# All matmuls of a convolution and gated MLP moved into two 64-row lanes

## Chip, cores and metric

One core of one Trainium2 chip. The metric is the device time of one execution in microseconds (us), the median of several executions. In the lines of the profile, PE is TensorE, PEld its weight loads, ACT is ScalarE, DVE is VectorE, POOL is GpSimd and SPq the DMA queue of SyncE.

## The reference

A depthwise causal convolution with 7 softmax-normalised taps per head, then `g = h * cos(h)` between two matrix products, over 32768 tokens:

```python
# convolution: x is 8 x 4096 x 192, weight is 8 heads x 7 taps; each head has 24 channels
w = softmax(weight)                       # over the 7 taps, 1e-9 in the denominator
out = np.einsum('hk,bskhg->bshg', w, x_unf)   # x_unf: the 7 last tokens of each token
# then, on out as 32768 x 192:
h = x @ w_in                              # 192 x 2048
g = h * np.cos(h)
return g @ w_out                          # 2048 x 192
```

## The kernel before

The 8 batches are handled as 4 pairs; `s` is the half of a pair. Every group of 448 tokens (a unit) is convolved on TensorE with a band matrix per head, copied to bf16, and transposed by DMA into `cT`. Then 512 steps, each 128 of the 2048 hidden columns for 2 x 512 tokens, run `up`, `sin` (ACT) and `mult` (DVE), and 19 steps later a sixteenth of the down-projection of 2 x 512 tokens. The 192 channels do not fit in 128 rows: channels 0 to 127 are a 128-row matmul, the other 64 are 64-row matmuls, one for each `s`, in the two halves of the array. The cuts of code below are shortened.

```python
h_pool = tc.tile_pool(name="hps", bufs=3, space=PSUM)   # 2 banks each
m_pool = tc.tile_pool(name="mps", bufs=1, space=PSUM)   # misc[0..1], convolution and down share them
...
def up(n):                                    # one step
    h = h_pool.tile([128, 2, T], FP32, name="h")
    for s in range(2):                        # 128 rows
        nc.tensor.matmul(out=h[:, s, :], lhsT=wA[:, f * 128:(f + 1) * 128], rhs=cT[b][:, s, t0:t0 + T],
                         start=True, stop=False)
    for s in range(2):                        # 64 rows: rows 0-63 for s=0, 64-127 for s=1
        p = slice(s * DR, (s + 1) * DR)
        nc.tensor.matmul(out=h[:, s, :], lhsT=wR[p, f * 128:(f + 1) * 128], rhs=cT[b][p, 2, t0:t0 + T],
                         start=False, stop=True)

def down(m):                                  # 8 matmuls of 128 rows and 192 columns
    ...
    for f in range(fh * 8, fh * 8 + 8):
        nc.tensor.matmul(out=bank[:, jj * D:(jj + 1) * D], lhsT=gs[i * NF + f][:, s, tk], rhs=wo[:, f, :],
                         start=(f == 0), stop=(f == NF - 1))

for k in range(6):
    conv_part(misc[k % 2])
for n in range(NSTEP + LAG):                  # LAG = 19
    m = n - LAG
    if n % 4 == 1: conv_part(misc[((m // 4) + 1) % 2])
    if n < NSTEP: up(n); sin(n)
    if m >= 0: down(m)
    if 1 <= n <= NSTEP: mult(n - 1)
```

The band matrices are built at the start by 8 x 7 DVE operations on seven masks.

## Time and profile before

| | before |
|---|---|
| median | 870.2 us (869.85 to 870.95, 3 runs) |
| TensorE, DVE, ACT busy | 93%, 80%, 74% |
| first up, first down, last down (start) | 53.8, 79.9, 864.8 us |
| one step in the full stretch | 1.52 us |

The last two rows are read from the starts of TensorE's instructions. The durations that the profile gives for matmuls overlap (247 ns on average for 192 columns, with starts 83 ns apart), so their sum exceeds the time on the clock. Only differences of starts give the pace. The prediction shows the lines.

### The profile page before, as it was taken

What the parts mean: (1) busy time and instruction counts of PE and PEld (TensorE: products, weight loads), DVE (VectorE), ACT (ScalarE), POOL (GpSimd) and SP (SyncE); (2) the same over time, 40 slices, a digit from 0 to 9 for tenths busy, and PEclk for the clock granted to TensorE, in tenths of its full rate; (3) what the DMA queues carried; (4) which work ended last, traced back from release to release, by engine and by line L of the source; (5) the groups of instructions that cost most, each with busy time, mean ns of one, the idle gap of its engine ahead of it and who ended that gap; (6) DMA issues with size and microseconds to landing.
All of it is one profiled execution on the core that took longest, in us unless ns stands there. A gap on an engine that the chain in (4) does not pass through costs nothing.

```text
span 869.1 us, 16182 instructions
## 1 busy us (share of the span) xinstructions
PE 811.0 (93%) x6744; PEld 474.2 (55%) x6744; DVE 694.6 (80%) x656; ACT 642.4 (74%) x685; POOL 59.5 (7%) x51
## 2 busy tenths in 40 slices
PE   0158999999999999999999999999999999999998
PEld 0013555555565556555555555555555555555557
DVE  1959888888888888888888888888888888888782
ACT  2048777777877777778777777787777778778773
POOL 1210010010000010100000000010000000000000
PEclk9999999999999999999999999999999999999999
DMA  7242332342332423433233334333332221011101
GB/s 208 76 109 67 93 101 59 94 117 78 93 90 76 126 65 88 110 90 90 76 90 98 88 79 122 88 84 84 94 91 76 59 55 37 20 37 38 38 31 61
DMA packets 128217, 71.20 MB, mean 82 GB/s; under 512 B 55440, under 2 KB 127632, under 8 KB 128144
## 3 DMA queue, kind: packets, MB, share of 16 engines
q1 hardware_dynamic: 128144, 70.18, 29.2%
q8 instruction: 52, 0.85, 0.4%
q14 instruction: 21, 0.17, 0.1%
HBM read 32.40 MB, written 25.17 MB: 66 GB/s over the span
## 4 chain that ended last, share of the span: by engine, by line
PE 91%; DVE 5%; DMA 2%; ACT 1%; issue 1%; SPq 0%; ACTq 0%
PE misc L262 45%; PE h L234 25%; PE h L238 18%; DVE band L144 3%; PE misc L161 2%; DVE g L249 2%; DMA st<-in_moe_w_in_dram 1%; PE misc L171 1%; DMA cT<-ct 0%; DVE ct L223 0%; ACT cos L244 0%; PE misc L168 0%; DVE band L142 0%; PE misc L204 0%; PE misc L163 0%
## 5 line engine op out<-in xcount | busy, mean ns | idle before, releaser
L249 DVE TENSOR_TENSOR g<-h,cos 128x1024 bf16<-128x1024 f32 x512 | 625.1, 1223 | 128.5 <-ACT cos L244 122.8
L244 ACT ACTIVATE cos<-h,halfpi 128x1024 bf16<-128x1024 f32 x512 | 569.6, 1113 | 172.4 <-PE h L238 167.3
L262 PE MATMUL misc<-wo,g 128*128 128x192 bf16 x4096 | 423.5, 247 | 0.0
L262 PEld LDWEIGHTS <-g 128*128 128x128 bf16 x4096 | 312.7, 98 | 111.6 <-issue 111.6
L234 PE MATMUL h<-cT,wA 128*128 128x512 bf16 x1024 | 305.7, 380 | 10.8 <-DMA cT<-ct 5.9
L238 PE MATMUL h<-cT,wR 64*128 64x512 bf16 x1024 | 200.1, 388 | 0.0
L238 PEld LDWEIGHTS <-wR 64*128 64x128 bf16 x1024 | 49.1, 93 | 217.7 <-issue 217.7
L234 PEld LDWEIGHTS <-wA 128*128 128x128 bf16 x1024 | 88.3, 98 | 15.0 <-DMA cT<-ct 6.6
L100 POOL CAST xb<-xw 128x1536 bf16<-128x1536 f32 x32 | 46.9, 1465 | 483.4 <-DMA xw<-in_x_dram 453.9
L267 ACT COPY osb<-misc 128x384 f32<-128x384 f32 x128 | 60.2, 470 | 10.3 <-PE misc L262 10.3
L161 PE MATMUL misc<-xb,band 128*128 128x96 bf16 x360 | 28.8, 211 | 37.2 <-DVE band L144 36.9
L223 DVE CAST ct<-misc 112x512 bf16<-112x512 f32 (+1 forms) x74 | 50.8, 687 | 10.6 <-PE misc L163 0.7
L161 PEld LDWEIGHTS <-band 128*128 128x128 bf16 x360 | 22.6, 100 | 39.2 <-DVE band L144 37.5
L221 ACT CAST ct<-misc 112x512 bf16<-112x512 f32 (+1 forms) x38 | 21.7, 572 | 27.0 <-PE misc L163 27.0
L144 DVE SCALAR_TENSOR_TENSOR band<-mask,wn,band 128x128 bf16<-128x128 bf16 x48 | 21.4, 445 | 1.7
L171 PE MATMUL misc<-xb,band 128*128 128x192 bf16 x72 | 12.4, 252 | 3.5 <-DVE halfpi L276 2.1
L163 PE MATMUL misc<-xb,band 128*128 128x32 bf16 x72 | 13.1, 182 | 2.2 <-DVE band L144 2.2
L129 DVE TENSOR_REDUCE wsum<-wex 128x8 f32<-128x56 f32 x1 | 0.2, 210 | 13.8 <-ACT wex L127 13.8
L95 POOL CAST xb<-xw 128x1536 bf16<-128x1536 f32 x4 | 5.9, 1463 | 61.6 <-DMA xw<-in_x_dram 43.3
L115 ACT CAST wA<-st 128x1024 bf16<-128x1024 f32 x2 | 2.1, 1044 | 10.1 <-DMA st<-in_moe_w_in_dram 10.1
L163 PEld LDWEIGHTS <-band 128*128 128x128 bf16 x72 | 7.2, 101 | 2.4 <-DVE band L144 2.4
L168 PE MATMUL misc<-xb,band 128*128 128x128 bf16 x36 | 8.0, 222 | 0.3 <-ACT ct L221 0.2
(26 smaller groups left out, 30.6 us busy)
## 6 DMA issues: line engine op xcount, KB each, us to landing
xw<-in_x_dram SPq DMA_DIRECT2D x64, 384.0 KB, 4.1
out_dram<-osb SPq DMA_DIRECT2D x64, 384.0 KB, 2.6
xw<-in_x_dram SPq DMA_DIRECT2D x8, 336.0 KB, 4.2
cT<-ct SPq DMA_TRANSPOSE x112, 2.4
st<-in_moe_w_out_dram SPq DMA_DIRECT2D x2, 768.0 KB, 8.9
st<-in_moe_w_in_dram SPq DMA_DIRECT2D x2, 512.0 KB, 9.1
st<-in_moe_w_in_dram SPq DMA_DIRECT2D x4, 256.0 KB, 7.1
xw<-in_x_dram SPq DMA_DIRECT2D x8, 60.0 KB, 2.4
```

Of the source, the lines that this page charges most:

```text
L100: nc.gpsimd.tensor_copy(out=xb, in_=xw)
L144: nc.vector.scalar_tensor_tensor(out=band[:, h, :], in0=mask[:, k, :], scalar=wn[:, h, k:k + 1], in1=band[:, h, :], op0=ALU.mult, op1=ALU.add)
L161: nc.tensor.matmul(out=ps[:, :, h * G:(h + 1) * G], lhsT=band[:, h, :], rhs=xb[:, s, 0:nb, h * G:(h + 1) * G], start=True, stop=True)
L171: nc.tensor.matmul(out=ps[:, :, :, h * G - DA:(h + 1) * G - DA], lhsT=band[:, h, :], rhs=xr[:, :, :, h * G:(h + 1) * G], start=True, stop= ...
L221: nc.scalar.copy(ct[0:rows, 0:cols], bank[0:rows, 0:cols])
L223: nc.vector.tensor_copy(out=ct[0:rows, 0:cols], in_=bank[0:rows, 0:cols])
L234: nc.tensor.matmul(out=h[:, s, :], lhsT=wA[:, f * 128:(f + 1) * 128], rhs=cT[b][:, s, t0:t0 + T], start=True, stop=False)
L238: nc.tensor.matmul(out=h[:, s, :], lhsT=wR[p, f * 128:(f + 1) * 128], rhs=cT[b][p, 2, t0:t0 + T], start=False, stop=True)
L244: nc.scalar.activation(out=cos, in_=hs[n], func=AF.Sin, bias=halfpi, scale=1.0)
L249: nc.vector.tensor_tensor(out=g, in0=hs.pop(n), in1=cs.pop(n), op=ALU.mult)
L262: nc.tensor.matmul(out=bank[:, jj * D:(jj + 1) * D], lhsT=gs[i * NF + f][:, s, tk], rhs=wo[:, f, :], start=(f == 0), stop=(f == NF - 1))
L267: nc.scalar.copy(osb[i][:, 2 * p:2 * p + 2, :].rearrange("p a d -> p (a d)"), bank[:, 0:2 * D])
```

## The change

Its intent is that TensorE never changes its row mode, that is between 128-row and 64-row matmuls. The time lost at such a change is called a drain below. All of them become 64-row matmuls in two lanes, rows 0 to 63 and rows 64 to 127, which alternate in the program. In the up-projection each lane takes one `s` and has its own PSUM bank. In the convolution and the down-projection the two lanes hold the two halves of one sum, so they first write one bank each and then trade banks. A trade waits for a one-element GpSimd memset that waits for the last matmul before it. The order of work comes from a string that is repeated once per 8 steps. The band goes to DRAM as rows and comes back with each row shifted. The convolution now takes its PSUM from the three `h` buffers.

```diff
+    lane = (slice(0, L), slice(L, 128))          # L = 64
+    def lanes(a, b, after=None):
+        todo, at, ins = [list(a), list(b)], [0, 0], None
+        while todo[0] or todo[1]:
+            k = 0 if at[0] <= at[1] else 1       # the lane that is behind
+            ...
+            ins = nc.tensor.matmul(out=o, lhsT=w, rhs=r, start=start, stop=stop, skip_group_check=True)
+            if after is not None:
+                order(ins, after); after = None
+        return ins
+    def changeover(end):
+        ins = nc.gpsimd.memset(mark, 0.0)
+        order(ins, end)
+        return ins
     def up(n):
-        (two 128-row matmuls, two 64-row matmuls)
+        lanes(*[[(h[:, l, :], w1[lane[l], c, fc], cT[b][lane[l], c, tk], T, c == 0, c == NCH - 1)
+                 for c in range(NCH)] for l in range(2)])     # NCH = 3
     def down(m):
-        (eight 128-row matmuls)
+        def half(bank, l):                       # four matmuls of lane l
+            return [(acc[bank][:, t * D:(t + 1) * D],
+                     gs[f][lane[l], s, (2 * bank + t) * 128:(2 * bank + t + 1) * 128], w2[lane[l], f % NF, :], D, ...)
+                    for f in (f0, f0 + 1) for t in range(2)]
+        end = lanes(half(flip, 0), half(1 - flip, 1), state.pop("turn") if j == 8 else None)
+        if j == 7:
+            state["turn"] = changeover(end)
@@ band
-    (masks, 8 x 7 DVE operations)
+    nc.scalar.dma_start(out=rows_d, in_=taps)
+    nc.scalar.dma_start(out=band, in_=dram(rows_d, rows_d.offset + 127, [[ROW - 1, 128], [1, H * 128]]))
@@ start and order
+    for c in range(1, 4):
+        load_w1(c)                               # DMA and a GpSimd cast each
+    for u in (2, 3):
+        load_unit(0, u)
+    opened = [conv_first() for _ in range(3)]
+    relay = changeover(opened[2][3])
+    prepare()
+    (second halves, copies, transposes)
+    for c in range(4):
+        load_w2(c)                               # DMA and a GpSimd cast each
+    emit("USM" * 2 + ("CUScMe" + "USM" * 3) * 3 + "USM" * 2 + "U")
+    while count["y"] < 2 * NI:
+        emit("dddSMdUdMSdUdMSdUMdSUdSMdUdSMCdcdeMUdSdUyxUMS")
```

U is an up, S the cosine, M the multiply, d half a former `down`, C and c the two halves of a convolution, e its copy, x and y the stores of the two banks.

## The prediction

> **What bounds the kernel now.** I read the page from the top: engine shares, the chain that ended last, the groups. The engine line and the chain say TensorE:
>
> ```profile
> PE 811.0 (93%) x6744; PEld 474.2 (55%) x6744; DVE 694.6 (80%) x656; ACT 642.4 (74%) x685; POOL 59.5 (7%) x51
> ...
> PE 91%; DVE 5%; DMA 2%; ACT 1%; issue 1%; SPq 0%; ACTq 0%
> ```
>
> A busy TensorE is not a full one, so next come the groups and the waits. L234 and L238 are the up-projection (128 rows, then two 64-row pieces), L262 the down-projection, L249 and L244 the elementwise pair:
>
> ```profile
> L249 DVE TENSOR_TENSOR g<-h,cos 128x1024 bf16<-128x1024 f32 x512 | 625.1, 1223 | 128.5 <-ACT cos L244 122.8
> L244 ACT ACTIVATE cos<-h,halfpi 128x1024 bf16<-128x1024 f32 x512 | 569.6, 1113 | 172.4 <-PE h L238 167.3
> ...
> L238 PEld LDWEIGHTS <-wR 64*128 64x128 bf16 x1024 | 49.1, 93 | 217.7 <-issue 217.7
> ```
>
> DVE and ACT wait for PE, not the reverse. And the weight load of L238 sits still for 217.7 us with nothing to wait for. The timeline of TensorE in the middle of the run shows why (first column the start, second how long, both in us):
>
> ```profile
> 400.53 0.83 PE L262 MATMUL misc<-wo,g 128*128 128x192 bf16 x8
> 401.20 0.59 PE L234 MATMUL h<-cT,wA 128*128 128x512 bf16 x2
> 401.73 0.39 PE L238 MATMUL h<-cT,wR 64*128 64x512 bf16 x2
> 402.05 0.83 PE L262 MATMUL misc<-wo,g 128*128 128x192 bf16 x8
> 402.72 0.59 PE L234 MATMUL h<-cT,wA 128*128 128x512 bf16 x2
> ```
>
> Take starts, not durations. One step is 402.72 - 401.20 = 1.52 us: eight L262 in 0.67 us (83 ns each), L234 to L238 in 0.53 us, L238 to L262 in 0.32 us. Instruction by instruction in the trace, the second L234 starts 215 ns after the first (the streaming of 512 columns), but the first L238 comes 311 ns after the second L234: 96 ns more. The two L238 start 3 ns apart and run side by side, and the next L262 comes 319 ns later: 104 ns more than their 215 ns. So each step loses **0.20 us** where the array goes from 128 rows to 64 and back.
>
> The table by stretches gives the rest:
>
> ```profile
> 0.00:54.00 54.00, 4.87 (x31) 2.63 (x31) 27.45 (x74) 8.06 (x9) 8.74 (x12) 1.00 0.51 139
> 54.00:80.00 26.00, 21.13 (x109) 6.55 (x109) 22.43 (x21) 21.68 (x21) 3.83 (x3) 1.00 0.32 85
> 80.00:400.00 320.00, 320.00 (x2707) 188.50 (x2706) 268.54 (x238) 252.23 (x270) 25.12 (x20) 1.00 0.33 90
> ```
>
> (PE, weight loads, DVE, ACT, GpSimd, then clock, DMA share and GB/s.) Until 54 us TensorE does almost nothing: the band matrices are being built on DVE (48 instructions of 445 ns, after an exponential that queues behind weight casts on ACT until 18.8 us), then the first transposes land. From 54 to 80 us the pipeline fills, and DVE sets the pace. From 80 us TensorE has no gap up to 852 us; the last 160 L262 take 13.3 us. This adds up: 493 steps x 1.518 = 748 us, plus 24 us of convolution, is 772 = 852 - 80.
>
> **What the Trainium skill says.** "TensorEngine Tiling (Array Packing)", Key Properties: changing the tiling mode drains the TensorE. The trace agrees: 96 and 104 ns. The same page, Gotcha 1: different row tiles cannot access the same PSUM bank at once. That is why the change makes the lanes trade banks; nothing in this trace tests it. "TensorE: Matmul & The Clock Gate", Part 3, The mechanism: tiles in different row groups run together, about 4 ns apart. Agrees: 3 ns. The same section lets weight loads be pulled ahead of running matmuls where row groups differ, and Part 2 adds: or if they go to the background weight buffer. At 128 rows the trace shows it (the load for the next matmul starts 2 ns after the present one); in 64-row lanes no stretch of this trace has two matmuls of one lane in a row, so there it is **not shown**. This is the main risk.
>
> **The change part by part.**
>
> *Removed: the drains.* All matmuls become 64-row. 493 steps x 0.200 us = 99 us of TensorE time in the full stretch.
>
> *Lanes.* A U (up) has 3 matmuls of 512 columns in each lane: 3 x 215 = 0.648 us. A d (half as many columns of down as a step had) has 4 of 192 columns in each lane, 4 x 83 = 0.335 us, and each step has two. So a step is 0.648 + 0.670 = 1.318 us against 1.518. Matmuls go from 12 to 22 a step, but with pairs 3 ns apart and 24-column ones 25 ns apart in the trace, issue is no bound. The convolution stays at some 0.44 us for 2 x 512 columns in two lanes.
>
> *One pass of the order string* is 16 d, 8 U, one C and c: 16 x 0.335 + 8 x 0.648 + 0.44 = 10.98 us of TensorE. Is anything else longer? A cos takes 1113 ns, but starts 1.01 us after the one before where work is queued; 8 x 1.01 + a conv copy of about 1.0 + a store of 0.47 = 9.6 us of ACT. A multiply takes 1223 ns, but four of them in a row at 62.64 to 67.17 us give 1.13 us each; 8 x 1.13 + 0.45 = 9.5 us of DVE. Both are 13% below TensorE, though neither can be called idle.
>
> *PSUM buffers.* h has still three, and now the convolution uses them too. A buffer is held for 0.65 (U) + 0.21 (end of stream to ACT) + 1.11 + 0.03 + 1.22 + 0.05 = 3.27 us, a convolution for some 2.0 us: (8 x 3.27 + 2.0) / 3 = 9.4 us a pass. I walked the string by hand with these times: the tightest places are C and the U after it, where the buffer comes free within 0.02 us of its use; the rest have 0.14 to 0.8 us to spare. So the string fits, with little play. I add 0.1 us a pass for slips: 6 us.
>
> *The GpSimd marks.* A bank trade needs PE to GpSimd to PE, a few tenths of a us (a small memset is 0.10 us). At the eighth d a U of 0.65 us lies between, at the convolution a d of 0.335 us. Hidden, or nearly so; GpSimd is 7% busy.
>
> *Start.* Now the exponential waits for the weights alone (4.8 us), seven small DVE operations of about 0.2 us replace the mask and band work, and two DMAs through DRAM follow. With 2.4 to 4 us each (the landings of small DMAs on the page), band is there at about 16 us instead of 45 us. But the first conv is not the first up: the relay mark is on GpSimd behind the casts of four weight chunks, and each of these has 0.79 MB to load, since both lanes need a copy. Inputs before it are 0.89 + 0.79 + 4 x 0.79 = 4.8 MB; the old start moved 2.5 MB in 13 us, so 25 us, and 28 with the band's own traffic. Then three second halves, copies, and three transposes of double size (now 1.2 us of issue each, so about 2.4) with two x loads ahead of them on the queue: first U at about 38 us instead of 54. Gain 16 us.
>
> *Fill.* 17 steps and 3 convolutions before the first d instead of 19 steps and 5. DVE's pace, 17 x 1.13, or the buffers', gives 20 us. First d at 58 us.
>
> *Sum.* From then on TensorE has 495 U, 1024 d, 50 convolutions: 321 + 343 + 22 = 686 us. End of matmuls 58 + 686 + 6 = 750 us; the last store takes 4 us in the trace of before (865 to 869). 754 us in the span; with the odd microsecond between span and measured time and the tail of d's a little better covered, I say **752 us**, 14% less than 870.2.
>
> **Rivals.**
>
> *A: lanes expose their weight loads.* If a load in a lane has to wait for that lane's own matmul, each of the 16 x 4 + 8 x 3 + 8 = 96 matmuls of a lane in a pass costs perhaps 25 ns more (24-column matmuls with their loads are 25 ns apart, so one load takes no longer). 2.4 us a pass, 64 passes, 154 us: about 900 us, slower. For it: no evidence of prefetch in 64-row mode here. Against it: prefetch at 128 rows, and 64-row loads as short (93 ns) as 128-row ones (98 ns).
>
> *B: a new wait takes the drain's place.* Buffers or ACT and DVE stall TensorE, since everything now stands at 86% or more. A slip of 0.5 us a pass is 32 us: 780 us. The missing slack at C speaks for it; the string, evidently laid out for these times, against.
>
> *C: the start does not get shorter*, since the doubled w_in traffic replaces the band's work: 768 us. Or it gets better than I think (w_in lands sooner, first U at 28 us): 742 us.
>
> *D: double rate in lanes does not hold at 192 columns with a weight load each.* It would be like A.
>
> **Range and chances.** C and a small B give 728 to 790 as the 8-in-10 range. A or D at full size is what could make it slower than 870; I give that 4%, within 2% another 3%, faster by over 2% 93%.
>
> **What would show it.** In the new trace: pairs of matmuls 3 ns apart and pairs 83 or 215 ns apart without the 96 and 104 ns steps; passes of some 11 us; idle time of TensorE before C and U put down to DVE or ACT below 0.2 us a pass; first up-matmul near 38 us; DVE and ACT at about 90% in the full stretch. The prediction is wrong if pairs come at 105 ns or more (A, D), if TensorE waits for h over 0.5 us a pass (B), or if waits for GpSimd marks show up on TensorE.

## The result

| | before | changed |
|---|---|---|
| median | 870.58 us (869.85 to 871.15, 4 runs) | 760.17 us (759.12 to 760.4, 4 runs) |
| ratio | | 0.873 (95%: 0.8715 to 0.8745) |
| first up | 53.8 us | 33.3 us |
| first down | 79.9 us | 65.5 us |
| last down (start) | 864.8 us | 754.1 us |

So 20.5 us went from the start, the fill between first up and first down took 6.2 us more (32.3 against 26.1), and the stretch from first to last down shrank from 784.9 to 688.6 us, by 96.3 us. The page of the changed kernel, engine shares, chain and two groups:

```profile
PE 709.8 (94%) x12064; PEld 518.3 (68%) x12064; DVE 645.2 (85%) x592; ACT 589.8 (78%) x639; POOL 85.7 (11%) x247
...
PE 91%; DMA 4%; DVE 2%; ACT 1%; issue 1%; POOL 1%; SPq 1%; POOLq 0%; ACTq 0%
...
L309 DVE TENSOR_TENSOR g<-h,cos 128x1024 bf16<-128x1024 f32 x512 | 609.9, 1221 | 45.7 <-ACT cos L304 33.8
L304 ACT ACTIVATE cos<-h 128x1024 bf16<-128x1024 f32 x512 | 515.0, 1025 | 113.2 <-PE h L191 95.3
```

TensorE is still the bound, with 1.8 times as many matmuls. DVE used to wait 122.8 us for the cosine and now waits 33.8 us. Next, the timeline of TensorE in the middle of the run (start, length, then the group):

```profile
300.29 0.82 PE L191 MATMUL acc<-w,g 64*128 64x192 bf16 x16
300.95 0.81 PE L191 MATMUL h<-cT,w 64*128 64x512 bf16 x6
301.60 0.49 PE L191 MATMUL acc<-w,g 64*128 64x192 bf16 x8
301.93 0.81 PE L191 MATMUL h<-cT,w 64*128 64x512 bf16 x6
302.58 0.82 PE L191 MATMUL acc<-w,g 64*128 64x192 bf16 x16
```

Sixteen matmuls of 192 columns (two d) start within 0.66 us, 83 ns for each pair. An up takes 0.65 us, 215 ns for each pair. Nothing is lost between groups. The starts of the y stores are 11.02 us apart in the passes with a convolution and 10.46 us in those without.

The start and the fill are read from the timeline of the first 66 us:

```profile
28.10 1.46 PE L191 MATMUL h<-xb,band 64*128 64x192 bf16 x20 [7.22 <-POOL mark L201]
...
33.27 0.61 PE L191 MATMUL h<-cT,w 64*128 64x512 bf16 x2 [3.71 <-DMA cT<-ct]
...
44.89 0.82 POOL L169 CAST w<-so 128x768 bf16<-128x768 f32 x1 [1.15 <-DMA so<-in_moe_w_out_dram]
45.66 0.09 POOL L201 MEMSET mark<- 1x1 f32 x1
...
45.80 0.61 PE L191 MATMUL h<-xb,band 64*128 64x192 bf16 x6 [5.56 <-POOL mark L201]
...
52.10 0.40 PE L191 MATMUL h<-xb,band 64*128 64x64 bf16 x8
...
58.25 0.40 PE L191 MATMUL h<-xb,band 64*128 64x128 bf16 x6
```

Twice TensorE stood still for a GpSimd mark, 7.2 and 5.6 us. The second time the mark is a 0.09 us operation queued behind a cast that waited for its DMA. The last two lines show the rhythm of the fill: two convolutions 6.15 us apart, with four ups between them.

### The profile page after: what moved, and what is told of

It is laid out like the page before. It is cut to its first block, busy times and chain, and to the rows that moved or that the text cites. A ratio compares the mean times of both kernels' runs of the same rounds, so it can differ in the third digit from the quotient of the medians.

```text
span 758.5 us, 26895 instructions
## 1 busy us (share of the span) xinstructions
PE 709.8 (94%) x12064; PEld 518.3 (68%) x12064; DVE 645.2 (85%) x592; ACT 589.8 (78%) x639; POOL 85.7 (11%) x247
## 4 chain that ended last, share of the span: by engine, by line
PE 91%; DMA 4%; DVE 2%; ACT 1%; issue 1%; POOL 1%; SPq 1%; POOLq 0%; ACTq 0%
PE h L191 46%; PE acc L191 44%; DMA st<-in_moe_w_in_dram 2%; DVE g L309 2%; DMA so<-in_moe_w_out_dram 1%; DMA xw<-in_x_dram 1%; ACT cos L304 1%; SPq L282 0%; POOL w L163 0%; POOL w L169 0%; ACT ct L274 0%; SPq L158 0%; ACT osb L343 0%; DVE osb L343 0%; SPq L98 0%
## 5 line engine op out<-in xcount | busy, mean ns | idle before, releaser
L309 DVE TENSOR_TENSOR g<-h,cos 128x1024 bf16<-128x1024 f32 x512 | 609.9, 1221 | 45.7 <-ACT cos L304 33.8
L304 ACT ACTIVATE cos<-h 128x1024 bf16<-128x1024 f32 x512 | 515.0, 1025 | 113.2 <-PE h L191 95.3
L191 PE MATMUL acc<-w,g 64*128 64x192 bf16 x8192 | 428.1, 243 | 1.3 <-ACT osb L343 0.8
L191 PEld LDWEIGHTS <-g 64*128 64x128 bf16 x8192 | 353.2, 94 | 101.8 <-issue 1.2
L191 PE MATMUL h<-cT,w 64*128 64x512 bf16 x3072 | 410.8, 379 | 10.3 <-DMA cT<-ct 5.0
L191 PEld LDWEIGHTS <-w 64*128 64x128 bf16 x3072 | 148.7, 94 | 89.3 <-issue 16.8
L191 PE MATMUL h<-xb,band 64*128 64x192 bf16 (+4 forms) x800 | 45.3, 230 | 32.9 <-DMA band<-rows_d 19.4
L274 ACT CAST ct<-h 112x1024 bf16<-112x1024 f32 x51 | 51.6, 1013 | 25.8 <-PE h L191 20.6
L343 DVE COPY osb<-acc 128x384 f32<-128x384 f32 x64 | 35.7, 558 | 38.4 <-PE acc L191 38.3
L113 POOL CAST xb<-xw 128x512 bf16<-128x512 f32 x102 | 60.1, 618 | 3.5 <-DMA xw<-in_x_dram 2.6
L343 ACT COPY osb<-acc 128x384 f32<-128x384 f32 x64 | 30.4, 475 | 11.1 <-PE acc L191 11.1
```

The lines of the kernel that those rows point to most:

```text
L113: nc.gpsimd.tensor_copy(out=xb[:, :, :, ch], in_=xw[:, :, :, ch])
L191: ins = nc.tensor.matmul(out=o, lhsT=w, rhs=r, start=start, stop=stop, skip_group_check=True)
L274: copy(out=ct[0:W], in_=ps[0:W])
L304: nc.scalar.activation(out=cos, in_=hs[n], func=AF.Sin, bias=math.pi / 2.0, scale=1.0)
L309: nc.vector.tensor_tensor(out=g, in0=hs.pop(n), in1=cs.pop(n), op=ALU.mult)
L343: copy(out=osbs[k][:, 2 * bank:2 * bank + 2, :].rearrange("p a d -> p (a d)"), in_=acc[bank][:, 0:2 * D])
```

## The experiments

Theory: the row-mode changes were what the change removed in the full stretch, two of some 100 ns in each step. Rivals: the lanes or the order string are faster for another reason; the gain is mostly the start. On the side: does the trade of banks cost anything, does the order matter, and what held the fill? All twelve kernels gave correct results.

### One part undone: the down-projection in 128 rows

```diff
-        end = lanes(half(flip, 0), half(1 - flip, 1), ...)
+        for f in (f0, f0 + 1):
+            for t in range(2):                   # bank `flip`, all 128 rows, no trade
+                nc.tensor.matmul(out=acc[flip][:, t * D:(t + 1) * D], lhsT=gs[f][:, s, tok], rhs=w2[:, f % NF, :], ...)
```

> The changed kernel with one part undone: the down-projection again in 128-row matmuls (bank 0 in the first eight d, bank 1 in the second), so the same columns streamed, no bank trade there, and half the matmuls; ups and convolution stay in lanes. Theory (the gain is the absent drains): one pass of the order string now changes the row mode 18 times at about 0.10 us, 1.8 us, 50 such passes and 12 of 1.4 us: 107 us more, about 867 us, steps of some 100 ns between h and acc matmuls again. Rival (lanes are faster for another reason, such as shorter weight loads or the better order string, start and fill): time stays within 20 us of 760.

Measured: 866.39 us (865.76 to 867.18, 4 runs), ratio to before 0.9955 (0.9935 to 0.9974). Nearly the whole gain is gone, though start, string, convolution and up-projection are the new ones. TensorE in the middle of the run:

```profile
300.60 0.82 PE L191 MATMUL h<-cT,w 64*128 64x512 bf16 x6
301.35 0.50 PE L326 MATMUL acc<-w,g 128*128 128x192 bf16 x4
301.79 0.82 PE L191 MATMUL h<-cT,w 64*128 64x512 bf16 x6
```

The same up takes 0.75 us up to the next start, not 0.65, and the same d 0.44 us, not 0.33. A pass is 12.81 us against 11.02: 1.79 us for 18 changes, **99 ns each**. The lanes as such are not faster.

### The mode changes removed from the kernel before by padding

```diff
-            p = slice(s * DR, (s + 1) * DR)
-            nc.tensor.matmul(out=h[:, s, :], lhsT=wR[p, ...], rhs=cT[b][p, 2, t0:t0 + T], ...)
+            nc.tensor.matmul(out=h[:, s, :], lhsT=wR[s][:, ...], rhs=cT[b][:, 2, t0:t0 + T], ...)
             # wR[s]: zeros in the other half's rows
```

> The kernel before with the two 64-row matmuls of a step made 128-row ones: their weights padded with zeros in the other half's rows. No mode change is left in the up and down loop, but each step streams 512 columns more. Theory: minus 0.200 us of drains, plus 0.215 us of streaming less rounding (1.524 against 1.518 us a step): 873 us, that is the same. Rival (the 0.2 us is no mode drain but a wait that belongs to these matmuls' operands): it stays, and the step is 1.73 us, about 980 us.

Measured: 872.53 us (871.35 to 874.23, 4 runs), ratio to before 1.0024 (1.0004 to 1.0044). TensorE in the middle:

```profile
401.74 0.59 PE L237 MATMUL h<-cT,wA 128*128 128x512 bf16 x2
402.17 0.59 PE L240 MATMUL h<-cT,wR 128*128 128x512 bf16 x2
402.60 0.82 PE L264 MATMUL misc<-wo,g 128*128 128x192 bf16 x8
```

All 0.43 us: the drains are gone from both borders and have been paid for with one more serial matmul. A drain pair (0.20 us) costs about as much as 512 columns (0.215 us), so here one can only gain by dropping the drains and keeping the two halves side by side. That is what the lanes do.

### The new band alone, in the kernel before

The mask and band operations of the kernel before were replaced by the taps, the DRAM write and the shifted read, as in the diff of the change.

> The kernel before with one part of the change alone: band rows written to DRAM and read back as shifted rows, in place of the mask and band work on DVE. Theory: band is there by about 16 us instead of 45, the first up comes at about 35 us instead of 53.8, and nothing later changes: about 852 us. Rival (weights, x loads and transposes hold the start anyway): 862 us or more.

Measured: 852.65 us (851.38 to 853.81, 4 runs), ratio to before 0.9793 (0.9775 to 0.9812). First up at 36.1 us instead of 53.8:

```profile
36.09 1.01 PE L234 MATMUL h<-cT,wA 128*128 128x512 bf16 x2 [8.51 <-DMA cT<-ct]
```

Nothing later changed: the stretch from first to last down is the same within 0.1 us, and the end of the span came 17.1 us earlier (869.1 to 852.0). So the start is a gain of its own, about 15% of the whole.

### Lanes in blocks instead of alternating

```diff
-            k = 0 if at[0] <= at[1] else 1
-            if not todo[k]:
-                k = 1 - k
+            k = 0 if todo[0] else 1              # all of lane 0, then all of lane 1
```

> The changed kernel with the matmuls of each group issued lane by lane (all of lane 0, then all of lane 1) instead of alternating. Theory (matmuls start strictly in program order, and two overlap only when neighbours in the stream are in different lanes): of the 6 matmuls of an up only two pairs at the borders overlap, 4 slots of 215 ns in place of 3, a down group 6 slots of 83 ns in place of 4; a pass 15.6 us against 11.0, about 1050 us. Rival (the lanes have queues of their own and sort themselves out): 760 us. Other rival (no overlap at all across a change of lane): 1440 us.

Measured: 761.19 us, one run, state unknown. My theory failed and the first rival's number came. The program of TensorE was compared and really has three or four matmuls of lane 0 and then as many of lane 1 in the full stretch. The timeline is nevertheless that of the alternating kernel:

```profile
300.11 0.84 PE L189 MATMUL acc<-w,g 64*128 64x192 bf16 x16
300.77 0.83 PE L189 MATMUL h<-cT,w 64*128 64x512 bf16 x6
301.42 0.51 PE L189 MATMUL acc<-w,g 64*128 64x192 bf16 x8
```

Single starts of the down-projection are some 20 and 63 ns apart in turn, where the alternating kernel mostly has 1 to 4 and 79. Lane 1 starts 20 ns after lane 0 and keeps pace with it, although three matmuls of lane 0 stand before its first one in the program. Matmuls of different row groups therefore start out of program order. The alternation in the change's `lanes` is not what makes the lanes overlap. That the lanes have queues of their own, as the rival says, is not shown by this; the next run tests it.

### Longer blocks

The same, with every run of d collected first: up to 16 matmuls of lane 0 ahead of lane 1 in the full stretch, and 32 in the last two passes.

> The changed kernel with every run of d in blocks: first all its lane 0 matmuls with their weight loads, then all of lane 1. Runs are two to four d in the full stretch (up to 32 instructions of lane 0 ahead of lane 1) and eight d in the last two passes (64 instructions ahead). The earlier run in short blocks kept both lanes busy 20 ns apart. Theory (the lanes run apart as far as a window of some tens of instructions reaches): the full stretch stays at 11.0 us a pass, lane 1 starting some 100 ns late at most; total 760 to 765. Rival (the earlier result holds only for a handful of instructions): blocks of four d lose up to 1 us each, 800 us or more.

Measured: 841.11 us, one run, state unknown (its granted clock was 1.0). The theory failed. The rival, that the overlap reaches only a handful of instructions and the total is 800 us or more, held. A pass is 12.27 us against 11.02, and the last two passes, all d, take 9.8 and 10.2 us against 6.7 and 6.5. The second half of the last pass in the timeline:

```profile
831.08 4.19 PE L189 MATMUL acc<-w,g 64*128 64x192 bf16 x64 [0.27 <-POOL mark L199]
```

One after the other, 64 would take 5.3 us at 83 ns; fully side by side, 2.65 us. These are not two blocks of 32: the kernel also ends a run at each C and c, so the program has 16 and 16, then 4 and 4, then 12 and 12. The single starts, laid beside this program, show how far the overlap reaches. Lane 0 runs alone until its 13th matmul; lane 1's first starts 9 ns later, and the lanes run together for the three of lane 0 that are left. Then lane 1 runs alone until its 13th, and lane 0's next block starts 9 ns later. In the half before, with 32 and 32, lane 1 starts 9 ns after lane 0's 29th. In each case three earlier matmuls of the other lane were still to start. The rule "a matmul may start once at most three earlier ones have not" gives all 64 starts within 0.07 us; with two or four instead of three, some are 0.19 or 0.31 us off. It also fits the run before: in blocks of four, three are left after the first matmul, so nothing is lost. The rule is read from the last pass of this one run; what else the longer passes of the full stretch lose was not taken apart.

### Nothing between the two halves of a convolution

The order string has `Ccdd` where it had `Cdcd`.

> The changed kernel with the order Ccdd in place of Cdcd: nothing for TensorE to do while GpSimd passes the mark of the convolution's bank trade. This measures the trade by itself. Theory (end of stream to GpSimd about 0.2 us, memset 0.09, back to TensorE about 0.1): TensorE waits some 0.3 to 0.4 us in each of 50 passes, 15 to 20 us, total 777. Rival (the trade is free or something else covers it): 760.

Measured: 776.11 us (775.86 to 776.81, 4 runs), 15.9 us above the changed kernel. A pass with a convolution is 11.35 us instead of 11.02, one without is unchanged at 10.46. One line of TensorE's timeline:

```profile
310.81 0.42 PE L191 MATMUL h<-xb,band 64*128 64x48 bf16 x13 [0.27 <-POOL mark L201]
```

A bank trade through GpSimd costs 0.33 us where nothing covers it. In the change a d of 0.33 us stands there and covers all of it. The trade is hidden, not free.

### A plain order string

`"ddUSM" * 5 + "dCdceUSMddUSMddUyxSM"` in place of the irregular string.

> The changed kernel with a regular order string, two d then U, S, M throughout, the convolution after the fifth: same work on every engine, another order. Theory (three h buffers with a hold of about 3.3 us leave so little play that the irregular string is needed): TensorE waits for h about 0.25 us a pass at the up after the convolution, about 775 us. Rival (TensorE is bound whatever the order): 760.

Measured: 852.86 us (852.41 to 853.41, 4 runs). The direction was right and the size far off: 1.8 us a pass lost, not 0.25. One pass in the timeline (in brackets: idle before, and what ended it):

```profile
404.98 1.01 ACT L274 CAST ct<-h 112x1024 bf16<-112x1024 f32 x1 [1.51 <-PE h L191]
...
406.95 2.35 DVE L309 TENSOR_TENSOR g<-h,cos 128x1024 bf16<-128x1024 f32 x2 [2.22 <-PE h L191]
...
408.22 0.82 PE L191 MATMUL h<-cT,w 64*128 64x512 bf16 x6 [0.65 <-DVE g L309]
...
409.82 0.82 PE L191 MATMUL acc<-w,g 64*128 64x192 bf16 x15 [0.71 <-DVE osb L343]
```

ACT stood 1.51 us waiting for the convolution that it had to copy next, while a cosine was already due behind that copy. I had overlooked that the fill leaves one up ahead, so every S in the string belongs to the up before the last one. The lag then passes down to DVE, to `h` and to the bank store. (The next run tests this.)

### The plain order with the cosine ahead of the copy

`"ddUSM" * 5 + "dCSMdceUddUSMddUyxSM"`.

> The plain order of the earlier run with one thing moved: the cosine of the up before the convolution is issued to ACT ahead of the convolution's copy, not behind it. In the plain order ACT stood idle 1.5 us a pass for the convolution with a cosine ready behind it, DVE then 2.2 us, and TensorE waited 0.65 us for h and 0.71 us for the acc store. Theory (the loss of the plain order comes from ACT's program order, which passes down to DVE and TensorE): the wait for h goes, that for the store stays at about 0.6 us; 805 to 815 us. Rival (three h buffers cannot carry a regular order): 840 or more.

Measured: 796.41 us (796.23 to 797.24, 4 runs), some 9 us better than the range I gave. The two lines of its table of waits (in total, times, longest) that bear on this:

```profile
PE acc L191 <- DVE osb L343: 14.4, 50, 0.3
PE h L191 <- DVE g L309: 4.6, 8, 0.9
```

All eight waits for `h` lie before 66 us, so in the full stretch TensorE only waits for the store on DVE, once a pass. A pass is 11.66 us. Moving the letters SM won 56 us of the 93 that the plain order had cost. The M moved too, but DVE's own order is unchanged by it; only ACT's is another. So most of that loss was ACT's program order and not the number of buffers. The irregular string is worth the other 36 us.

### The fill: casts of the output weights later

```diff
-    (each load_w2 casts on GpSimd at once)
-    emit("USM" * 2 + ("CUScMe" + "USM" * 3) * 3 + "USM" * 2 + "U")
+    emit("USM" * 2 + ("CUScMe" + "USM" * 3) * 3)
+    for c in range(4):
+        cast_w2(c)                               # GpSimd, four staging buffers
+    emit("USM" * 2 + "U")
```

> The changed kernel with the four GpSimd casts of w_out moved behind the three convolutions of the fill (their loads stay where they were, with four buffers). In the changed kernel the first mark of the fill stood behind these casts and TensorE waited 5.6 us for it. Theory (GpSimd's own order lengthened the fill): that wait goes, the first down comes some 6 to 8 us earlier than 65.5 us, total 753. Rival (DVE and the three h buffers set the fill's length anyway): 2 us or less, 758.

Measured: 754.58 us (754.41 to 754.86, 4 runs), 5.6 us less than the changed kernel. The first down came at 59.7 us instead of 65.5. This is about the wait of 5.6 us for the mark. The fill is now 26.4 us, and its rhythm has not changed:

```profile
44.46 0.40 PE L198 MATMUL h<-xb,band 64*128 64x64 bf16 x8 [0.72 <-DVE g L316]
...
50.62 0.40 PE L198 MATMUL h<-xb,band 64*128 64x128 bf16 x6 [0.72 <-DVE g L316]
```

Four ups and a convolution take 6.16 us: four times DVE's 1.13, and 1.6 us that the convolution adds. In these 1.6 us DVE stands idle twice, 0.84 and 0.60 us, for a cosine. I put them down to the convolution's turn in the three `h` buffers (an up waits 0.88 us for its copy), but the copy also takes 1.0 us of ACT ahead of the next cosine, and no run separates the two.

### The start: the relay mark earlier

The opening convolutions and their mark were put ahead of the casts of the third and fourth weight chunk.

> The changed kernel with the opening convolutions and their relay mark put ahead of the casts of the third and fourth weight chunk on GpSimd. Theory (the relay behind these casts is what delays the first up): mark at 21 us instead of 28, first up up to 6 us earlier, total 754. Rival (the transposes then queue behind the x loads that sit ahead of them): first up 2 us earlier, total 758.

Measured: 758.04 us (757.61 to 758.62, 4 runs). The first up came at 32.2 us, 1 us earlier. The rival holds, with 1 us in place of its 2: with this wait gone, the transposes stand behind the loads ahead of them. Issued at 24.2 us, the first lands 8.0 us later, against 3.5 us in the changed kernel and in the next run, which has them ahead of the x loads.

### Towards a better version

Both mends together, the first transposes ahead of the x loads, and the first convolution of the fill at the sixth up:

> A version meant to beat both: the relay ahead of the later weight casts, the first transposes ahead of the x loads, the casts of w_out behind the fill's convolutions, and these convolutions starting at the sixth up instead of the third. Theory (start and fill are bound by these waits; the full stretch of 689 us stays): first up at about 27 us, first down at about 49, end at 742 in the span, 744 measured. Rival (the DMA queue bounds the start, DVE and buffers the fill): 752 or more.

Measured: 752.26 us (751.39 to 752.85, 5 runs), ratio to before 0.8643 (0.8631 to 0.8655). I had expected 744; the rival's number, 752 or more, came. First up at 26.5 us as expected, but first down at 57.4: GpSimd stood 9.6 us on the last weight chunk, and the fill's first convolution waited 5.2 us for its casts behind it.

```profile
34.20 1.46 POOL L164 CAST w<-st 128x1536 bf16<-128x1536 f32 x1 [9.61 <-DMA st<-in_moe_w_in_dram]
...
37.11 0.24 PE L198 MATMUL h<-xb,band 64*128 64x192 bf16 x1 [3.04 <-POOL xb L114]
...
39.51 0.48 PE L198 MATMUL h<-xb,band 64*128 64x192 bf16 x4 [2.17 <-POOL xb L114]
```

The next version loads x units 2 and 3 before the last two weight chunks, puts the transposes before these chunks, and casts the last chunk after the fill's first convolution:

> The best version so far had its fill held by DMA order: x units 2 and 3 came behind the weight chunks, and GpSimd stood 9.6 us on the last chunk. Here x units 2 and 3 are loaded ahead of the last two weight chunks, the transposes before these chunks, and the cast of the last chunk comes after the first convolution of the fill. Theory (order of loads and of GpSimd's work held it, not the amount): first up at about 27 us, first down at about 50, span 743, 745 measured. Rival (the queue has no more to give; first up moves later by what the x loads take): 752.

Measured: **749.44 us** (748.93 to 749.62, 4 runs), ratio to before 0.8606 (0.8593 to 0.8619), against 0.873 for the changed kernel. It is correct, and the best of all. First up at 28.3 us, first down at 54.8. I had expected 745: the fill again took 26.6 us and not 23. This fits 17 x 1.13 for DVE, 3 x 1.6 for the convolutions, and 2.6 us in which the first up's three pairs wait for the three transposes one by one.

## Why the prediction was right

The time was forecast at 752 us and measured at 760.2, inside the range. The mechanism of the full stretch came as forecast. That the errors of start and fill partly cancel is luck, as the end of this list shows. The steps one by one:

- **Drains, 99 us: right.** The stretch between first and last down shrank by 96 us; putting the drains back cost 106 us for 1068 changes (18 in 50 passes, 14 in 12; the last two passes, all d, have none to speak of), 99 ns each. Padding them away changed nothing, as it should.
- **Pace of the lanes, 83 and 215 ns a pair: right.** Rivals A and D did not come. Weight loads are hidden in 64-row lanes too, which the trace of before could not show.
- **A pass of 10.98 us and 0.1 for slips: right.** It measured 11.02. Rival B did not come with this string, but the plain orders show how near it is: 11.66 and 12.79 us.
- **The last two passes: a little short.** I counted them at 5.3 us; they took 6.7 and 6.5. No up is left there to cover the trades and stores; with the down-projection in 128 rows, without a trade, the last pass took 5.3 us. So the tail was not "a little better covered", as the forecast's last step has it.
- **Marks, "Hidden, or nearly so; GpSimd is 7% busy": right in the full stretch, wrong in the fill.** Share of busy time was the wrong measure. One mark stood in GpSimd's program behind four casts that waited for DMAs: 5.6 us, shown by moving the casts.
- **Start, first up at 38 us: 5 us too late.** The relay mark came at 28.0 us as I had worked out, but from there to the first up it took 5.3 us, where I gave 10. The band was there at 19.4 us and not at 16. That cost nothing here, since the mark came later; with the mark early, the opening convolutions wait for the band until 19.6 us.
- **Fill, "gives 20 us": the mis-sized term.** It took 32.3 us. 5.6 us are the mark. The version with late casts still took 26.4 us, 6.4 more than forecast. That is two things I left out: each of the three convolutions adds 1.6 us (by its turn in the `h` buffers or its copy on ACT, see above), and the three matmul pairs of the first up wait for one transpose each, 2.5 us from 33.3 us on. With the 19.2 us of 17 x 1.13 this makes 26.5.

The two errors in start and fill have opposite signs; without the first, the forecast would have been 13 us low and not 8.

## What to carry to other kernels

Before you count matmuls, look for borders between row modes in the stream of starts: here each cost 99 ns, and the 1068 of the run with the down-projection in 128 rows 12% of its time. Two lanes need not alternate in the program as long as their blocks are short: here blocks of four lost nothing, blocks of 16 did. An engine's low busy share does not make a small synchronising operation on it cheap; what counts is what stands before it in that engine's program. Where several engines work in order near their limits, two letters in the order of the program can be worth several per cent: here 56 of 853 us.

## What the Trainium skill lacked or had wrong

- "TensorE: Matmul & The Clock Gate", Part 3, The mechanism, says that matmuls are strict FIFO in start and end, with no reordering. With the two lanes in blocks of three or four, matmuls of lane 1 started 20 ns after lane 0's first, ahead of lane 0 matmuls earlier in the program (761.2 us, as fast as alternating). In blocks of 12, 16 and 32 a matmul started ahead of three earlier ones of the other lane and no more, as read from the last pass (841.1 us). Whether ends also leave program order was not tested.
- "TensorEngine Tiling (Array Packing)", Key Properties, says that a change of tiling mode drains, without a figure. Here it was 99 ns for a change between 128 and 64 rows, the same in both directions within 10 ns.
- No page that I read has a figure for a bank trade between row tiles. One through a GpSimd memset cost 0.33 us where nothing covered it.
